# Block attention and a top-1 mixture of experts on one core: where a head pair's two value steps stand in its string of TensorE phases

## The chip, the core and the metric

The kernel runs on one core of a Trainium2 chip. The metric is the device time of one execution in microseconds (us), lower is better. Engines are named as the profile names them: PE is TensorE's matrix multiply and PEld its weight load, DVE is VectorE, ACT is ScalarE, POOL is GpSimd, SP is SyncE, which here only issues transfers. PSUM is the memory that PE writes and that DVE and ACT empty.

## The reference

```
scores = q @ k.T / sqrt(64)                     # 8 batches, 8 heads, 576 positions, depth 64
scores = where(block_i >= block_j, scores, -1e9)       # blocks of 64
attn   = exp(scores - max) / (sum + 1e-9)
x      = (attn @ v), heads side by side          # 4608 tokens x 512
e      = argmax(x @ w_gate);  gate = softmax(x @ w_gate)[e]
eom    = sigmoid(x @ w_output_gate)
out    = gate * eom[e] * (relu(x @ w1[e]) @ w2[e])     # 8 experts, 512 -> 1024 -> 512
```

## The kernel before

The program has two stages. The first, up to about 340 us, is the attention; the second multiplies the sorted tokens by the experts' weights and isn't touched by the change.

The attention goes over 32 head pairs (8 batches, 4 pairs of heads each, `hp` 0 to 3). The work of one pair runs through three turns of the function `attend`: in its first turn the scores and their exponentials, in the next the turning (transposing) of the exponentials, in the third the product with the values. So one call of `attend` works on three pairs at once, and a string of letters sets the order in which PE gets their pieces. PE's order is taken as the code issues it, but for pieces whose buffer the scheduler sees as still taken, behind which it may let the next ones pass. DVE, ACT and POOL get the order that a list scheduler makes of the rest.

- **S** is a step of `softmax`, for the newest pair. Four steps: S1 has query tiles 0 and 1, S2 tile 2, S3 tile 3, S4 the last tile of both heads. Each writes scores into a buffer of the pool `ps_s` (two buffers, each two banks of PSUM; L356 scores, L364 mask, L406 for S4). DVE then takes the maximum (L375), ACT the exponential (L368, for S4 L412). A `ps_s` buffer is free again when its last exponential has been taken, so S1 uses the buffer of the S3 before it, S3 that of S1, S2 that of S4, S4 that of S2.
- **F** is a step of `flip`, for the pair before. F1 to F3 each turn sixteen 64x64 pieces into the pool `ps_f` (one buffer of two banks, L436); ACT and DVE copy one bank each to `pT` (L439). F4 turns two pieces (L460) into a buffer of the pool `ps_t`, which ACT copies (L461).
- **V** is a step of `values`, for the pair before that. V1 multiplies the first two key tiles (L474, eight matmuls that fill one buffer of `ps_t`); V2 the other two, and the last query tile into another buffer of `ps_t` (L474, L487). ACT then copies the one (L481), DVE the other (L491).
- **t** is a tick of `finish_batch`, which normalises a finished batch, writes its rows and routes its tokens (L499 to L689). Its pieces also go through `ps_t`, which has only two buffers, in turn. A batch's ticks spread over four calls, which I name by the `hp` of their newest pair (that of S): in the pair with hp 2 the two parts of the gate's product (L538, copied by ACT at L542), in that with hp 3 rows and logits (L510, L513, L554, L555), in hp 0 three more blocks of rows, in hp 1 the ranks (L638 to L655).
- **.** is the pair's other work: it issues loads, splits of q and k on POOL, and the transposing transfers on SP (L163) which make `qk`, the operand of the scores three pairs on.

Of the kernel before, what the change touches and what calls it, by code (L numbers as in the profile page):

```python
# [26 lines left out]
def block_attention_top1_moe(  # L27
# [12 lines left out]
    B, H, S, D = q.shape  # L40
# [388 lines left out]
    def flip(probs, pT):  # L429

        def group(c0, srcs):
            ps = two_banks()
            for i, src in enumerate(srcs):
                for h in range(2):
                    rows = slice(64 * h, 64 * h + 64)
                    nc.tensor.transpose(ps[:, h, 64 * i:64 * i + 64], src[rows], ident[rows, rows])  # L436
            to = pT.rearrange("p h (s c) -> p h s c", c=P)[:, :, c0:c0 + 10:3]
            one, other = (
                copy(to[:, h], ps[:, h].rearrange("p (s c) -> p s c", c=P))  # L439
                for h, copy in enumerate((nc.scalar.copy, nc.vector.tensor_copy))  # L440
            )
            tc.add_to_no_dep_group(f"turned{one.ins.name}", one.ins)
            tc.declare_no_dep(other.ins, group=f"turned{one.ins.name}", reason="halves in separate banks")

        def keys(pt, j):
            return pt[:, P * j:P * j + P]

        def both(t, n):
            return [keys(probs[t][:, ab], j) for j in range(n) for ab in range(2)]

        pl = probs[LAST]
        group(3, both(3, 4))
        yield
        group(2, both(2, 3) + [keys(pl, 2), keys(pl, 3)])
        yield
        group(1, both(1, 2) + [pl[:, S0:S0 + P], keys(pl, 3), keys(pl, 0), keys(pl, 1)])
        yield
        ps = ps_t.tile([P, 512], F32, name="ps_t")
        for i, src in enumerate(both(0, 1)):
            nc.tensor.transpose(ps[:, P * i:P * i + P], src, ident)  # L460
        nc.scalar.copy(pT[:, :, 0:P].rearrange("p h (a n) -> p a h n", a=2), ps[:, 0:2 * P].rearrange("p (a h n) -> p a h n", a=2, h=2))  # L461
        yield

    def values(hp, pT, vv, vl, xT):

        a0 = 2 * hp
        pa = ps_t.tile([P, 512], F32, name="ps_t")
        for j0, j1 in ((0, 2), (2, LAST)):
            for j in range(j0, j1):
                for ab in range(2):  # L470
                    o = slice(64 * ab, 64 * ab + 64)
                    x = turned_at(j, j)
                    m = LAST - j
                    nc.tensor.matmul(  # L474
                        pa[o, P * j:S0].rearrange("p (t h n) -> p t h n", h=2, n=64), vv[:, j, a0 + ab],
                        pT[:, :, x:x + P * m].rearrange("p h (t n) -> p t h n", n=P)[:, :, :, o],
                        start=(j == 0), stop=(j == LAST - 1),
                    )
            if j0 == 0:
                yield  # L480
        nc.scalar.copy(xT[:, hp, 0:S0], pa)  # L481
        pm = ps_t.tile([P, 512], F32, name="ps_t")
        for j in range(NT):
            for ab in range(2):
                o = slice(64 * ab, 64 * ab + 64)
                x = turned_at(j, LAST)
                nc.tensor.matmul(  # L487
                    pm[o, 0:64], vv[:, j, a0 + ab] if j < LAST else vl[:, a0 + ab], pT[:, ab, x:x + 64],
                    start=(j == 0), stop=(j == LAST),
                )  # L490
        nc.vector.tensor_copy(xT[:, hp, S0:S], pm[:, 0:64])  # L491
        yield
# [584 lines left out]
    def step(g, n=1):  # L1077
        for i in range(n):
            next(g, None)

    def attend(soft, extra=None):

        nxt, flipped, valued = [], iter(()), iter(())
        if flips:
            hp, b, probs, sums, xT, vab = flips.pop()
            pT = sb.tile([P, 2, NPT], F32, name="pT")
            nxt = [(hp, b, pT, vab, sums, xT)]
            flipped = flip(probs, pT)
        if prods:
            hp, b, pT, vab, sums, xT = prods.pop()  # L1090
            valued = values(hp, pT, *vab, xT)
        else:
            hp = None
        def tick():
            for g in list(later):
                if next(g, later) is later:
                    later.remove(g)

        turns = iter(range(4))
        with tc.manual_schedule(engines=ENG):  # L1100
            for x in "S.F.SVFSV.FttSFtt.":
                if x == "S":
                    step(soft)
                elif x == "V":
                    step(valued)
                elif x == "F":
                    step(flipped)
                elif x == "t":
                    tick()
                elif extra is not None:  # L1110
                    extra(next(turns))

        if hp == NP - 1:
            later.append(finish_batch(b, *sums, xT))
        prods.extend(nxt)
# [4 lines left out]
    for p in range(NPR):  # L1120
# [42 lines left out]

        probs = {}
        attend(softmax(p, *sums, probs), others)
        flips.append((hp, b, probs, sums, xT, values_of[b]))
        if p == CP:
# [22 lines left out]
    ps_t.release()  # L1190
    ps_t = ctx.enter_context(tc.tile_pool(name="ps_y", bufs=4, space=PSUM, reuse_waits="tile"))
    attend(iter(()), both_x)
    hp, b, pT, vab, sums, xT = prods.pop()
    ended = values(hp, pT, *vab, xT)
# [126 lines left out]
```

## Time and profile before

| | |
|---|---|
| three runs | 765.82 us in the median (763.86 to 768.5) |
| the profiled execution | 760.66 us, span of its instructions 759.1 us |
| PE busy over the span | 710.0 us, 94% |
| DVE, ACT, POOL busy | 522.8, 489.9, 317.2 us (69%, 65%, 42%) |
| mean granted TensorE clock | 0.994 of full |

Busy time of PE is time in which at least one matmul is in flight. The 1.6 us between the span and the execution's own time lie outside the instructions.

### The profile page before, as it was taken

The page shows a single profiled execution, that of the slowest core. Times are in us where ns is not written, and L with a number is a line of the kernel's source. Part 1 is how long each engine was busy: PE and PEld are TensorE (multiplying, and loading weights), DVE is VectorE, ACT ScalarE, POOL GpSimd, SP SyncE. Part 2 cuts the span into 40 slices and gives each one's busy share as a digit, 9 for nine tenths or more (in the row PEclk, how much of TensorE's full clock was granted, in tenths as well). Part 3 has the DMA queues.
Part 4 walks back from the last instruction along what each step waited for, and adds up shares of the span by engine and source line. Part 5 has one row for each costly group of instructions (what it writes and reads, how often), then busy time and mean ns, then how long its engine had stood idle before and what let it go on. Part 6 is the DMA issues. An engine that isn't in the chain of part 4 may idle for free. (4 is left out here: it accounts for less than half of the span.)

```text
span 759.1 us, 20344 instructions
## 1 busy us (share of the span) xinstructions
PE 710.0 (94%) x7967; PEld 498.6 (66%) x7990; DVE 522.8 (69%) x873; ACT 489.9 (65%) x1081; POOL 317.2 (42%) x377
## 2 busy tenths in 40 slices
PE   6989899999998999988999999999999999999994
PEld 4766576767776676656577666667666666766661
DVE  5866777878786878787849657765576665766630
ACT  4877687878787787854348656656566566566530
POOL 4091669677675783135365224132123232110111
PEclk9999999999999999999999999999999999999998
DMA  6979999998999996369565885947899679623501
GB/s 161 170 142 211 199 223 171 168 195 164 218 163 196 181 160 163 108 220 235 109 146 120 276 263 126 287 128 243 253 315 283 145 225 294 100 37 101 191 30 44
DMA packets 238359, 136.04 MB, mean 179 GB/s; under 512 B 194096, under 2 KB 210544, under 8 KB 238256
## 3 DMA queue, kind: packets, MB, share of 16 engines
q1 hardware_dynamic: 229440, 115.11, 67.2%
q0 software_dynamic: 8272, 19.29, 8.4%
q8 instruction: 65, 1.06, 0.7%
q14 instruction: 38, 0.31, 0.2%
q10 hardware_dynamic: 544, 0.26, 0.1%
HBM read 122.23 MB, written 19.73 MB: 187 GB/s over the span
## 5 line engine op out<-in xcount | busy, mean ns | idle before, releaser
L1035 PEld LDWEIGHTS <-w1b 128*128 128x128 f16 (+1 forms) x2112 | 182.5, 98 | 26.1 <-issue 3.0
L1035 PE MATMUL ps_s<-xt,w1b 128*128 128x256 f16 (+3 forms) x1824 | 182.1, 261 | 0.5 <-DVE w1b L920 0.4
L1062 PE MATMUL ps_t<-w2b,hh 128*128 128x512 bf16 (+1 forms) x585 | 175.9, 379 | 0.0
L920 DVE TENSOR_TENSOR w2b<-w2f,w2b 128x1024 bf16<-128x1024 f32 x76 | 88.0, 1220 | 114.6 <-ACT w2b L918 114.6
L375 DVE TENSOR_REDUCE nmx<-ps_s 128x1 f32<-128x512 f32 (+4 forms) x224 | 130.4, 618 | 17.6 <-PE ps_s L364 14.7
L368 ACT ACTIVATE pt<-ps_s,nmx 128x256 f32<-128x256 f32 (+3 forms) x256 | 131.9, 535 | 8.8 <-DVE nmx L375 8.7
L1066 POOL DMA_INDIRECT out_dram<-ys,ids x38 | 45.4, 1195 | 181.8 <-ACT ys L1065 118.1
L1062 PE MATMUL ps_t<-w2b,hl 128*128 128x512 f16 x304 | 115.2, 379 | 2.1 <-DVE hl L1044 1.0
L1065 ACT ACTIVATE ys<-ps_t,ids 128x512 f32<-128x512 f32 x38 | 26.1, 687 | 135.0 <-PE ps_t L1062 115.5
L1062 PEld LDWEIGHTS <-hh 128*128 128x128 f16 x608 | 59.2, 98 | 66.8
L356 PE MATMUL ps_s<-qk 64*128 64x256 f16 (+1 forms) x1152 | 74.8, 255 | 17.0 <-DMA qk<-sp 11.0
L920 DVE TENSOR_TENSOR w1b<-w1f,w1b 128x1024 bf16<-128x1024 f32 x76 | 88.1, 1218 | 0.0
L439 DVE COPY pT<-ps_f 128x512 f32<-128x512 f32 x93 | 63.9, 688 | 33.5 <-PE ps_f L436 33.5
L474 PE MATMUL ps_t<-pT,vv 128*64 128x256 f32 (+3 forms) x512 | 83.8, 448 | 2.0 <-DVE xn L513 2.0
L918 ACT CAST w1b<-w1f 128x1024 f16<-128x1024 f32 x76 | 74.1, 1045 | 0.5 <-DMA w1f<-in_moe_w_dram 0.5
L887 POOL DMA_INDIRECT xg<-x_d,ids x38 | 53.1, 1397 | 49.8 <-DVE xr L1001 14.9
L918 ACT CAST w2b<-w2f 128x1024 f16<-128x1024 f32 x76 | 73.6, 1042 | 0.0
L356 PEld LDWEIGHTS <-qk 64*128 64x128 f16 x1152 | 50.2, 95 | 29.6 <-DMA qk<-sp 13.6
L439 ACT COPY pT<-ps_f 128x512 f32<-128x512 f32 x93 | 55.5, 596 | 19.3 <-PE ps_f L436 18.6
L436 PEld LDWEIGHTS ps_f<-ident,pt 64*128 64x128 f32 x1116 | 42.7, 139 | 25.0 <-issue 13.1
L436 PE MATMUL ps_f<-ident,pt 64*128 64x64 f32 x1116 | 54.6, 231 | 3.7 <-DVE pT L439 2.3
L689 POOL DMA_INDIRECT tab_d<-idg,sli x40 | 41.0, 1025 | 36.7 <-DVE sli L658 17.3
(213 smaller groups left out, 992.4 us busy)
## 6 DMA issues: line engine op xcount, KB each, us to landing
w1f<-in_moe_w_dram SPq DMA_DIRECT2D x76, 512.0 KB
w2f<-in_moe_w_dram SPq DMA_DIRECT2D x76, 512.0 KB
vv<-in_v_dram SPq DMA_DIRECT2D x64, 128.0 KB
x_d<-xn SPq DMA_DIRECT2D x32, 256.0 KB
natk<-in_k_dram SPq DMA_DIRECT2D x14, 512.0 KB
natq<-in_q_dram SPq DMA_DIRECT2D x28, 256.0 KB
hh<-in_moe_w_dram SPq DMA_DIRECT2D x4, 512.0 KB
hl<-in_moe_w_dram SPq DMA_DIRECT2D x4, 512.0 KB
```

The costliest lines, as they stand in the source:

```text
L356: nc.tensor.matmul(ps[:, ab, c:c + m], qk[rows, cq, P * t:P * t + P], cols(qk[rows, ck], x, kind), start=(i == 0), stop=(i == 2 and c + m ...
L368: last_exp[0] = nc.scalar.activation(probs[t][:, ab], ps[:, ab, c0:c0 + n], AF.Exp, bias=nmx[:, t, ab:ab + 1], accum_out=sums[:, t, 2 * hp ...
L375: last_max[0] = nc.vector.tensor_reduce(o, x, AX.X, ALU.max, negate=True)
L436: nc.tensor.transpose(ps[:, h, 64 * i:64 * i + 64], src[rows], ident[rows, rows])
L439: copy(to[:, h], ps[:, h].rearrange("p (s c) -> p s c", c=P))
L474: nc.tensor.matmul(pa[o, P * j:S0].rearrange("p (t h n) -> p t h n", h=2, n=64), vv[:, j, a0 + ab], pT[:, :, x:x + P * m].rearrange("p h ( ...
L887: nc.gpsimd.indirect_dma_start(out=xg[i % NXG][:, h], out_offset=None, in_=x_d[0:nx, :], in_offset=IOA(ap=ids[i][:, h, 0:1].bitcast(U32), ...
L918: nc.scalar.copy(hi, src)
L920: eng.tensor_tensor(lo, src, hi, ALU.subtract)
L1035: nc.tensor.matmul(ph[:, f4].rearrange("p (h n) -> p h n", n=P), wv[:, cc, f, :], xv[:, cc], start=(k == 0), stop=(k == 3 * KD - 1))
L1062: nc.tensor.matmul(py, hv[:, f, h], wv[:, f, :], start=(k == 0), stop=(k == 3 * KF - 1))
L1066: nc.gpsimd.indirect_dma_start(out=out, out_offset=IOA(ap=ids[i][:, h, 0:1].bitcast(U32), axis=0), in_=ys, in_offset=None, bounds_check=NT ...
```

## The change

The string in `attend` is another. Each step is issued as often as before; the order of S, F and V changes, and with it the four places of the other work.

```diff
-            for x in "S.F.SVFSV.FttSFtt.":
+            for x in "SF.VSF.VSF.ttSFtt.":
```

With their numbers the phases are, before and after:

```
S1 . F1 . S2 V1 F2 S3 V2 . F3 t t S4 F4 t t .
S1 F1 . V1 S2 F2 . V2 S3 F3 . t t S4 F4 t t .
```

On PE, in the middle of a pair, the program before has the end of S2's mask, V1, F2, and the start of S3 (`pt` and `plast` are exponentials, `vv` and `vlast` values):

```order
L364 LDWEIGHTS mrow
L364 MATMUL ps_s<-mneg,mrow 128x2x32
L474 MATMUL ps_t<-pT,vv 64x512 x2
L474 MATMUL ps_t<-pT,vv 64x384 x2
L436 MATMUL ps_f<-ident,pt_3192 128x64 x12
L436 MATMUL ps_f<-ident,plast_115 128x64 x4
L356 LDWEIGHTS qk
L356 MATMUL ps_s<-qk 128x256
```

The changed program has at this place the end of S2's mask, F2, the whole of V2, and the start of S3:

```order
L364 LDWEIGHTS mrow
L364 MATMUL ps_s<-mneg,mrow 128x2x32
L436 MATMUL ps_f<-ident,pt_3193 128x64 x12
L436 MATMUL ps_f<-ident,plast_115 128x64 x4
L474 MATMUL ps_t<-pT,vv 64x256 x2
L474 MATMUL ps_t<-pT,vv 64x128 x2
L487 MATMUL ps_t<-pT,vv 64x64 x8
L487 MATMUL ps_t<-pT,vlast_106 64x64 x2
L356 LDWEIGHTS qk
L356 MATMUL ps_s<-qk 128x256
```

V1 went from behind S2 to ahead of it, V2 from behind S3 to ahead of it; F2 follows S2 at once.

On DVE, in the pair with hp 3, the program before has F2's copy, S3's maxima, V2's copy, F3's copy, two pieces of the tick and S4's maximum:

```order
L439 COPY pT<-ps_f 128x4x128
L375 TENSOR_REDUCE nmx<-ps_s 128x1 x2
L491 COPY xT<-ps_t 128x64
L439 COPY pT<-ps_f 128x4x128
L513 TENSOR_TENSOR xn<-ps_t,rec 64x512
L555 TENSOR_TENSOR lh<-ps_t,rec 128x512
L375 TENSOR_REDUCE nmx<-ps_s 128x1
```

The changed program has there:

```order
L439 COPY pT<-ps_f 128x4x128
L491 COPY xT<-ps_t 128x64
L375 TENSOR_REDUCE nmx<-ps_s 128x1 x2
L439 COPY pT<-ps_f 128x4x128
L513 TENSOR_TENSOR xn<-ps_t,rec 64x512
L555 TENSOR_TENSOR lh<-ps_t,rec 128x512
L375 TENSOR_REDUCE nmx<-ps_s 128x1
```

Only V2's copy moved, ahead of S3's maxima; F3's copy and the tick's pieces still stand behind these maxima.

On DVE in the pair with hp 2 (L683 is a reciprocal that waits for POOL, L502 a small copy of the tick) the piece of the difference is:

```order
+L491 COPY xT<-ps_t 128x64
+L375 TENSOR_REDUCE nmx<-ps_s 128x1 x2
+L439 COPY pT<-ps_f 128x4x128
+L502 COPY sums<-ps_t 64x4
 L683 RECIPROCAL idg<-zs 128x5
-L491 COPY xT<-ps_t 128x64
-L439 COPY pT<-ps_f 128x4x128
-L502 COPY sums<-ps_t 64x4
 L546 RECIPROCAL rec<-rec 128x40
 L375 TENSOR_REDUCE nmx<-ps_s 128x1
```

The reciprocal that waits for POOL stands behind F3's copy and L502 now, and no longer ahead of V2's copy. ACT's order is the same in both programs in the steady pairs, POOL's throughout; on SP one store of rows changes places with one transposing transfer.

## Rows read from the trace of the kernel before

**Rows 1.** Busy us by stretch, one batch: length, engines' busy us, PEclk, DMA share, GB/s.

```profile
165.00:203.00 38.00, 36.97 (x607) 26.91 (x606) 30.82 (x63) 30.78 (x99) 27.21 (x38) 1.00 1.00 188
```

**Rows 2.** The waits of PE, whole span: waiting <- releaser: us in total, times, longest.

```profile
PE ps_s L356 <- DMA qk<-sp: 11.0, 7, 2.6
```

**Rows 3.** Timeline of PE, pair hp 3: start us, us, line, op.

```profile
158.59 0.67 PE L356 MATMUL ps_s<-qk 64*128 64x256 f16 x12
...
159.22 1.72 PE L474 MATMUL ps_t<-pT,vv 128*64 128x512 f32 x8
160.88 0.59 PE L436 MATMUL ps_f<-ident,pt 64*128 64x64 f32 x12
...
161.42 0.82 PE L356 MATMUL ps_s<-qk 64*128 64x256 f16 x12
162.08 0.19 PE L364 MATMUL ps_s<-mneg,mrow 64*128 64x64 bf16 x2
162.20 0.87 PE L474 MATMUL ps_t<-pT,vv 128*64 128x256 f32 x8
...
163.58 0.46 PE L436 MATMUL ps_f<-ident,pt 64*128 64x64 f32 x8
...
164.22 0.62 PE L510 MATMUL ps_t<-ident,xT 128*64 128x128 f32 x4
...
165.12 0.91 PE L406 MATMUL ps_s<-qk 128*128 128x256 f16 x9
165.86 0.41 PE L460 MATMUL ps_t<-ident,pt 128*128 128x128 f32 x2
166.21 0.28 PE L356 MATMUL ps_s<-qk 64*128 64x128 f16 x3
```

**Rows 4.** Timeline of DVE, the same pair.

```profile
162.31 1.29 DVE L375 TENSOR_REDUCE nmx<-ps_s 128x1 f32<-128x512 f32 x2
...
164.33 0.69 DVE L439 COPY pT<-ps_f 128x512 f32<-128x512 f32 x1 [0.41 <-PE ps_f L436]
164.94 0.67 DVE L513 TENSOR_TENSOR xn<-ps_t,rec 64x512 f32<-64x512 f32 x1
```

**Rows 5.** Timeline of PE, pair hp 0: F2 and S3.

```profile
171.20 0.59 PE L436 MATMUL ps_f<-ident,pt 64*128 64x64 f32 x12 [0.48 <-DVE pT L439]
...
172.16 0.83 PE L356 MATMUL ps_s<-qk 64*128 64x256 f16 x12 [0.24 <-ACT pt L368]
```

**Rows 6.** Timeline of PE behind pair hp 1: S1 and S2 of the next.

```profile
185.72 0.34 PE L356 MATMUL ps_s<-qk 64*128 64x128 f16 x6
...
187.25 0.67 PE L356 MATMUL ps_s<-qk 64*128 64x256 f16 x12 [0.28 <-ACT plast L412]
```

**Rows 7.** Timeline of PE, first pair: S3's mask, then the next pair's S1.

```profile
15.10 0.21 PE L364 MATMUL ps_s<-mneg,mrow 64*128 64x64 bf16 x2
...
17.73 0.34 PE L356 MATMUL ps_s<-qk 64*128 64x128 f16 x6 [0.77 <-ACT pt L368]
```

**Rows 8.** Timeline of all engines, pair hp 2: S3, its first exponential, L542, second L538.

```profile
151.95 0.82 PE L356 MATMUL ps_s<-qk 64*128 64x256 f16 x12
...
154.13 0.69 ACT L368 ACTIVATE pt<-ps_s,nmx 128x512 f32<-128x512 f32 x1
...
156.10 0.58 ACT L542 COPY lgT<-ps_t 128x512 f32<-128x512 f32 x1
...
157.06 0.32 PE L538 MATMUL ps_t<-xT,wg_bd 128*32 128x64 f32 x8
```

**Rows 9.** Timeline of PE, three stretches: the longest waits after 110 us.

```profile
116.84 1.07 PE L538 MATMUL ps_t<-xT,wg_bd 128*32 128x512 f32 x8 [1.22 <-DVE xT L491]
...
245.18 0.28 PE L356 MATMUL ps_s<-qk 64*128 64x128 f16 x3 [2.57 <-DMA qk<-sp]
...
265.54 0.34 PE L356 MATMUL ps_s<-qk 64*128 64x128 f16 x6 [0.79 <-DMA qk<-sp]
```

**Rows 10.** Timeline of POOL, pair hp 3: a split that waits for a transfer.

```profile
164.57 0.72 POOL L152 CAST sp<-natq 128x640 f16<-128x640 f32 x1 [3.51 <-DMA qk<-sp]
```

## The prediction

> **What bounds the kernel now.** I read the stretches first: one batch of the attention, four pairs, takes 38.0 us, of which PE is busy 36.97, DVE 30.8 and ACT 30.8 [rows 1]. In the middle of the attention PE is all but full, and what can be won there is about 1 us a batch. Then the waits of PE: the largest is S1 waiting for its `qk`, 11.0 us in seven places [rows 2]. Two of them are the S1 rows at 245.18 and 265.54 us [rows 9]; the other five lie in the first 100 us and take 11.0 - 2.57 - 0.79 = 7.6 us together. There a transfer sets the time, not PE's order. Then the timeline of PE, for the length of each phase as the difference of starts: S2 0.63, V1 1.66, F2 0.54, S3 0.78, V2 1.38, F3 0.64, the tick ahead of S4 0.9, S4 0.74, F4 0.35 [rows 3]. Last DVE and ACT, for how soon a buffer of PSUM is empty again.
>
> The second stage, from about 345 us on, is PE-bound and keeps its order; I carry it over unchanged. So the sum is over the attention alone.
>
> **What the change moves.** No instruction is added or removed, and V1 and V2 still lie between the same two F's. So the distance from F1 to F2 and from F2 to F3, which must cover the copies out of the single `ps_f` buffer, stays as it is. What changes is when S2 and S3 end: S2 by V1's 1.66 us later, S3 by V2's 1.38 us later, while F3, S4, F4 and the ticks stay in place. Behind S3's last matmul there used to be V2; now F3, S4, F4 and the next S1 and F1 follow with nothing between that needs no quick emptying.
>
> *S1 behind S3.* S1 takes S3's buffer. In the first pair no V has begun yet, and the trace shows the new order's spacing: S3's mask ends at 15.10 + 0.21 = 15.31, and S1 starts at 17.73 after a wait for ACT [rows 7]. So about 2.4 us must lie between. In the changed order S3's mask ends 0.85 us after S3 starts and F3 starts at 0.78; F3, S4 and F4 then take 0.64 + 0.74 + 0.35 = 1.73, so PE reaches S1 1.66 us after the mask [rows 3]. A tick between them adds 0.9 in hp 3 and as much or more in hp 0 and hp 2: enough there. In hp 1 the tick is a few small matmuls, and S1 waits. Bounds: 0 (the ranks' matmuls and a faster DVE fill it) to 0.76; I take 0.45, since DVE in the first pair was also busy with other work. Against this S2 has V1 ahead of it now and no longer waits for S4's exponential: the 0.28 of [rows 6] goes. Sum for hp 1: **+0.2**.
>
> The Trainium skill (Perfetto Trace Analysis, "Optimizing Tensor Performance") asks that independent matmul groups go round different PSUM banks, so that ACT or DVE empties one while the next group runs. The changed order still does so: S3 in one `ps_s` buffer, F3 in `ps_f`, S4 in the other `ps_s`, F4 in `ps_t`. By this rule alone every copy stays hidden, none of the waits of this part comes, and the sum is that of the faster rival below. The first pair's row goes round the same way and waits all the same, because the way round is shorter than the emptying; where they differ I go by the row.
>
> *F4 and the ticks behind S3's maxima, hp 3.* DVE's two maxima of S3 take 1.29 us, start 0.04 after the mask, and F3's copy stands behind them. Now that copy starts when F3 ends, 0.75 after F3's start (164.33 against 163.58) [rows 3, 4]. In the changed order it starts at 0.85 + 0.04 + 1.25 = 2.14 after S3's start, that is 1.36 after F3's: 0.6 later. The L513 behind it ends at 164.94 + 0.67 = 165.61 now; with some 0.15 for the signal F4, which needs that buffer of `ps_t`, could start at 165.76 and does at 165.86 [rows 3, 4]. The slack is 0.1, so F4 comes 0.5 late. The scheduler has let one matmul of S1 pass F4, and the two further ticks come behind S1. Bounds 0 and 0.6; I take **+0.4**.
>
> *hp 0.* S3 waits 0.24 for S1's exponentials, and starts 0.96 after F2 where 0.54 is the rule [rows 3, 5]. V2 between them ends this: -0.4. The wait of F2 for its copy (0.48) stays: DVE only swaps S1's maxima with a reduction of the tick, with the same sum ahead of F1's copy. Two blocks of rows then wait as in hp 3, +0.4. Sum: **0**.
>
> *hp 2.* The gate's second L538 needs the buffer that ACT empties at L542. L542 ends at 156.68, L538 starts at 157.06: slack 0.38 [rows 8]. S3's first exponential starts 2.18 after S3 now, behind V2's copy; it can start at 0.85 + 0.65 + 0.1 = 1.6 in the changed order, so with S3 1.38 later ACT's row comes 0.8 later. 0.8 - 0.38 = 0.42, and a little for the signal: **+0.5** (bounds 0, and 1.0 if ACT gains nothing). In the first batch the reciprocal that waits for POOL stood ahead of V2's copy and cost L538 1.22 us [rows 9]; it now stands behind what L538 needs. That place then has only the new wait: **-0.6**.
>
> A steady batch so costs 0.2 + 0.4 + 0 + 0.5 = +1.1 us.
>
> **The sum.** Up to about 100 us the five other waits for `qk`, 1.5 us in the mean, follow each other pair by pair, so what PE loses or gains there is swallowed. From there to the S1 at 245.18: hp 1 of the first batch +0.2, hp 2 -0.6, three batches at 1.1, hp 3 +0.4, together +3.3. That S1 waited 2.57 us for its transfer [rows 9], which I take to come when it came: +0.7 is left. The pairs up to 265.54 add 0.2, and the 0.79 waited there leaves 0.1. Behind it no `qk` is waited for: hp 2 +0.5, hp 3 +0.4, hp 0 nothing (DVE has the ticks' arithmetic there), hp 1 without a tick +0.3, hp 2 +0.5, the last hp 3 +0.4. The last `attend` follows DVE's work, which is the same; there the change puts F3 ahead of a step that waits for a load, -0.1. Total 0.1 + 2.0 = **+2.1 us**, on the profiled 760.66 that is 762.8. The median of the runs shown is 5.2 us above that execution, so I forecast 767.9, 0.3% above 765.82. The measurement can tell about 0.5%, 3.8 us, from no change: the forecast is "same", on the slow side.
>
> **Rivals.**
> - *The new waits are not swallowed, and F3 gets one in each pair (slower).* F2's copy on ACT now stands behind S2's exponentials, which are 1.66 us later. From S2 to F3 there are 0.63 + 0.54 + 1.38 + 0.78 = 3.33 us [rows 3]. The chain for S3's tile is 0.85 to the mask's end, 0.65 for one maximum, two exponentials at 0.68, 0.6 for a copy, some 3.5; S2's tile is a quarter narrower, so about 3.1. The slack is 0.2 in all of some 26 pairs. It decides when a copy or a small piece of a tick pushes ACT 0.2 us back: each further 0.2 costs 5 us. Besides, the transfers may come later too: POOL's splits wait for small results of DVE that now stand behind S4's maximum, up to 3 us later by the same working, against the 3.51 us that POOL waits for a transfer's end anyway [rows 10]; if these don't hide it, the 3.4 us swallowed above come back. For it: both margins are thin. Against it: both are positive in the rows. Time: 767.9 + 3.4 to 5 = 771 to 773.
> - *The gains stay and the late copies are hidden (faster).* hp 0 -0.4, hp 1 -0.28, over five batches, and the 1.22 of [rows 9]: -4.6 us, part of which turns into waits for `qk`. Time about 762. Against it: the slack of 0.1 at F4 and of 0.38 at L538 are far below the 1.38 us by which S3 comes later.
> - *The transfers alone set the pace.* A `qk` arrives 2.57 us late for 245.18; if all S1 from 165 us on are nearly bound by it, neither loss nor gain shows before the last 60 us: +2 or less, within the forecast's range of 765 to 770. The new order of SP is one swap and can't move it much.
>
> **Chances.** The forecast and the transfers' case 0.55 together, the slower rival 0.35, the faster 0.10. Range: from the faster rival's 762 to 774, the slower one's 773 and a little for the part of its waits that I couldn't bound; the likeliest case alone has 764.5 to 770.5. Faster by over 0.5% 0.09, within 0.5% 0.55, slower by over 0.5% 0.36.
>
> **What would show it.** In the profile after: a wait of S1 for ACT behind hp 1 (0.3 to 0.7 us), of F4 or the ticks for DVE in hp 3 and hp 0, of L538 for ACT in hp 2; the waits of rows 5 (S3's), 6 (S2's) and the 1.22 of rows 9 gone; the waits for `qk` at the places of 245 and 265 us smaller by what PE lost before; V's and F's lengths unchanged and the second stage as long as now. The prediction is wrong if F3 waits for ACT in most pairs, if DVE's F3 copy is not later against F3, or if the waits for `qk` move by more than PE's own delay.

## The result, and the profile after

The changed kernel takes 774.44 us in the median of four runs (772.06 to 776.32), the kernel before 765.58 (763.86 to 768.50): the ratio is 1.011 (1.0068 to 1.0152), slower by more than the 0.5% that can be told from no change. The forecast was 767.9, the range 762 to 774. In four more measurements of the same two kernels, in which both ran on the same chip, the ratio is 1.0070 (1.0037 to 1.0103) on a first chip, 1.0043 (1.0010 to 1.0076) and 1.0040 (1.0010 to 1.0070) on a second, and 1.0110 (1.0063 to 1.0156) on a third. What sets the third apart is the main finding below. The ratios leave out slow runs, more than 1.5% over the fastest of the same kernel, so they lie a little off those of the medians, which are of all runs. On which chip the first measurement's runs took place isn't known; three of its four runs of the kernel before were there ahead of the prediction, the fourth, 765.33 us, came with the result.

The profiled execution takes 772.06 us, its span is 770.4. Busy times of the whole span, and the stretch that answers to [rows 1] (length, busy us of PE, PEld, DVE, ACT, POOL, PEclk, DMA share, GB/s):

```profile
PE 718.9 (93%) x7990; PEld 504.8 (66%) x7990; DVE 517.3 (67%) x873; ACT 489.7 (64%) x1081; POOL 321.1 (42%) x377
...
165.00:203.00 38.00, 36.75 (x596) 26.70 (x594) 30.06 (x62) 30.36 (x98) 27.68 (x38) 1.00 1.12 193
```

A batch in the middle looks nearly as before: PE is busy 36.75 of 38 us, where it was 36.97. What the change did there is seen in single waits. The waits of PE over the whole span (compare [rows 2]: us in total, times, longest):

```profile
PE ps_s L356 <- ACT pt L368: 8.1, 10, 2.1
PE ps_s L356 <- DMA qk<-sp: 6.7, 5, 2.0
...
PE ps_s L356 <- issue: 1.9, 5, 0.5
...
PE ps_f L436 <- DVE mx L573: 1.4, 5, 0.3
PE ps_t L538 <- DVE sums L502: 1.2, 1, 1.2
...
PE ps_s L1035 <- issue: 1.0, 3, 0.4
```

The kernel before has, of these:

```profile
PE ps_s L356 <- ACT pt L368: 2.6, 7, 0.8
...
PE ps_s L356 <- issue: 0.2, 1, 0.2
```

S1 and S3 now wait 8.1 us for ACT, not 2.6; less is waited for `qk`; and there are rows that the kernel before hardly has: "issue", where PE stands still and no wait is recorded.

The timeline of PE in the pair with hp 3, from S3 on (before: [rows 3]), then of DVE there (before: [rows 4]):

```profile
164.03 0.83 PE L356 MATMUL ps_s<-qk 64*128 64x256 f16 x12
...
164.72 0.44 PE L436 MATMUL ps_f<-ident,pt 64*128 64x64 f32 x8
...
166.24 0.91 PE L406 MATMUL ps_s<-qk 128*128 128x256 f16 x9
167.15 0.21 PE L356 MATMUL ps_s<-qk 64*128 64x128 f16 x1
167.46 0.44 PE L460 MATMUL ps_t<-ident,pt 128*128 128x128 f32 x2
```

```profile
164.93 1.29 DVE L375 TENSOR_REDUCE nmx<-ps_s 128x1 f32<-128x512 f32 x2 [0.56 <-PE ps_s L364]
166.13 0.68 DVE L439 COPY pT<-ps_f 128x512 f32<-128x512 f32 x1
166.73 0.67 DVE L513 TENSOR_TENSOR xn<-ps_t,rec 64x512 f32<-64x512 f32 x1
```

F3's copy starts 166.13 - 164.72 = 1.41 us after F3, where it was 0.75; F4 starts 1.22 after S4, where it was 0.74, with a matmul of S1 ahead of it. The other places, in PE's timeline: the second L538 in hp 2, F2 in hp 0 (before: [rows 5]), S1 behind hp 1 ([rows 6]):

```profile
119.85 0.32 PE L538 MATMUL ps_t<-xT,wg_bd 128*32 128x64 f32 x8 [0.25 <-ACT lgT L542]
...
172.56 0.34 PE L436 MATMUL ps_f<-ident,pt 64*128 64x64 f32 x4 [0.27 <-DVE mx L573]
...
187.65 0.34 PE L356 MATMUL ps_s<-qk 64*128 64x128 f16 x6 [0.47 <-ACT pt L368]
```

S3's wait of [rows 5], S2's of [rows 6] and the 1.22 of [rows 9] are gone, as foretold. No F3 waits for ACT.

**Where the time went in this execution.** S4 of pair 27 starts 1.0 us later than before (283.63 against 282.62), S4 of pair 31 6.8 us later, the end 11.3 us later. So the loss between these two profiles stands at the end of the attention and behind it. In PE's timeline of pair 29:

```profile
304.45 0.35 PE L487 MATMUL ps_t<-pT,vlast 128*64 128x64 f32 x4 [0.39 <-issue]
305.17 0.41 PE L356 MATMUL ps_s<-qk 64*128 64x256 f16 x4 [0.36 <-issue]
305.92 0.27 PE L356 MATMUL ps_s<-qk 64*128 64x256 f16 x1 [0.34 <-issue]
306.64 0.38 PE L356 MATMUL ps_s<-qk 64*128 64x256 f16 x3 [0.45 <-issue]
307.36 0.27 PE L356 MATMUL ps_s<-qk 64*128 64x256 f16 x1 [0.34 <-issue]
308.06 0.39 PE L356 MATMUL ps_s<-qk 64*128 64x256 f16 x3 [0.43 <-issue]
```

One to four matmuls come every 0.72 us, although nothing is waited for: PE halts. The same is seen at L1035 from 352.2 to 353.6. The granted clock falls behind the halts of pair 29, and again in the hand-over to the experts (windows as above):

```profile
304.00:306.00 2.00, 0.91 (x12) 0.50 (x9) 0.69 (x1) 0.70 (x3) 1.44 (x2) 1.00 0.02 1
306.00:308.00 2.00, 0.83 (x5) 0.13 (x4) 0.00 (x0) 0.00 (x0) 1.95 (x3) 1.00 0.02 1
308.00:310.00 2.00, 1.94 (x26) 1.58 (x27) 1.71 (x4) 1.35 (x4) 0.81 (x1) 0.66 0.00 0
310.00:312.00 2.00, 2.00 (x22) 1.42 (x22) 1.16 (x2) 1.90 (x6) 0.00 (x0) 0.50 0.00 0
...
366.00:368.00 2.00, 0.39 (x5) 0.26 (x3) 2.00 (x4) 0.10 (x1) 1.70 (x2) 0.66 1.04 381
368.00:370.00 2.00, 2.00 (x16) 1.81 (x16) 1.15 (x2) 0.00 (x0) 0.98 (x2) 0.50 1.30 317
370.00:372.00 2.00, 2.00 (x20) 2.00 (x19) 1.77 (x3) 0.00 (x0) 0.00 (x0) 0.50 0.87 117
```

PE had been busy 0.91 and 0.83 us of 2 ahead of the first fall, and 0.39 of 2 ahead of the second. Then it worked at 0.5, which is 1.2 GHz, for 3.4 us from 308.6 on and for 6.8 us from 366.6 on. In the profile of before the clock is full in both places. Is this the change's doing?

### The profile page after: what moved, and what is told of

It is laid out like the page before. It is cut to its first block, busy times and chain, and to the rows that moved or that the text cites. A ratio compares the mean times of both kernels' runs of the same rounds, so it can differ in the third digit from the quotient of the medians.

```text
span 770.4 us, 20390 instructions
## 1 busy us (share of the span) xinstructions
PE 718.9 (93%) x7990; PEld 504.8 (66%) x7990; DVE 517.3 (67%) x873; ACT 489.7 (64%) x1081; POOL 321.1 (42%) x377
## 5 line engine op out<-in xcount | busy, mean ns | idle before, releaser
L1035 PEld LDWEIGHTS <-w1b 128*128 128x128 f16 (+1 forms) x2112 | 184.5, 99 | 27.5 <-issue 4.3
L1035 PE MATMUL ps_s<-xt,w1b 128*128 128x256 f16 (+3 forms) x1824 | 182.1, 261 | 0.3 <-DVE w1b L920 0.2
L1062 PE MATMUL ps_t<-w2b,hh 128*128 128x512 f16 x608 | 180.8, 379 | 0.0
L368 ACT ACTIVATE pt<-ps_s,nmx 128x256 f32<-128x256 f32 (+3 forms) x256 | 132.3, 530 | 43.4 <-DVE nmx L375 41.6
L1062 PE MATMUL ps_t<-w2b,hl 128*128 128x512 f16 x304 | 115.2, 379 | 1.2 <-DVE hl L1044 1.2
L1062 PEld LDWEIGHTS <-hh 128*128 128x128 f16 x608 | 59.2, 98 | 66.8
L356 PE MATMUL ps_s<-qk 64*128 64x256 f16 (+1 forms) x1152 | 78.3, 256 | 18.7 <-ACT pt L368 8.1
L356 PEld LDWEIGHTS <-qk 64*128 64x128 f16 x1152 | 46.7, 95 | 51.3 <-issue 35.6
L887 POOL DMA_INDIRECT xg<-x_d,ids x38 | 56.2, 1480 | 42.9 <-issue 15.0
L439 ACT COPY pT<-ps_f 128x512 f32<-128x512 f32 x93 | 54.4, 585 | 12.9 <-PE ps_f L436 11.3
L689 POOL DMA_INDIRECT tab_d<-idg,sli x40 | 41.0, 1025 | 46.7 <-DVE idg L683 19.7
L1043 ACT ACTIVATE hh<-ps_s 128x1024 f16<-128x1024 f32 (+1 forms) x44 | 39.7, 905 | 27.0 <-PE ps_s L1035 25.0
```

The source lines that it names most:

```text
L356: nc.tensor.matmul(ps[:, ab, c:c + m], qk[rows, cq, P * t:P * t + P], cols(qk[rows, ck], x, kind), start=(i == 0), stop=(i == 2 and c + m ...
L368: last_exp[0] = nc.scalar.activation(probs[t][:, ab], ps[:, ab, c0:c0 + n], AF.Exp, bias=nmx[:, t, ab:ab + 1], accum_out=sums[:, t, 2 * hp ...
L887: nc.gpsimd.indirect_dma_start(out=xg[i % NXG][:, h], out_offset=None, in_=x_d[0:nx, :], in_offset=IOA(ap=ids[i][:, h, 0:1].bitcast(U32), ...
L1035: nc.tensor.matmul(ph[:, f4].rearrange("p (h n) -> p h n", n=P), wv[:, cc, f, :], xv[:, cc], start=(k == 0), stop=(k == 3 * KD - 1))
L1062: nc.tensor.matmul(py, hv[:, f, h], wv[:, f, :], start=(k == 0), stop=(k == 3 * KF - 1))
```

## Experiments

In all that follows a *step* is the time from S4 of one pair to S4 of the next. Theory: the loss is made behind pair 26. Rival: each pair costs. Second rival: halts and late transfers come by chance or with the chip, and the change itself costs 2 to 4 us.

**The changed kernel again**, on the first chip and on the third.

> The changed kernel once more. If what its profile shows behind 300 us belongs to the program (matmuls that come in small groups from 304.4 to 308.1 us with nothing to wait for, and then the clock at 0.5 up to 312; the clock at 0.5 again from 367 to 373), a second profile has both at the same places and the ratio is again 1.007 to 1.015. If they were chance, the profile lacks them and the time is 4 to 8 us lower.

> The changed kernel a third time, on the chip of these runs. If its loss is what the steps between pairs show, +3 to +4 us (1.004 to 1.005); if it is the 8.9 us of the first measurement, 1.010 to 1.013.

On the first it gave 769.16 against 765.00 us, ratio 1.0070, and its profile has no halt in pair 29 and none at L1035. (It has one stall that no other profile shows: S1 of pair 18 waits 1.90 us at 187.9, and the clock is at half for 3.4 us from 188.8 on.) On the third it gave 778.74 against 772.23, ratio 1.0110: of the two cases expected there, the 8.9 us of the first measurement came and not the 3 to 4 us of the steps. On this chip the kernel before is slower too, and the profile has the halts of pair 29 again:

```profile
307.85 0.35 PE L487 MATMUL ps_t<-pT,vlast 128*64 128x64 f32 x4 [0.37 <-issue]
308.56 0.48 PE L356 MATMUL ps_s<-qk 64*128 64x256 f16 x5 [0.36 <-issue]
310.00 0.41 PE L356 MATMUL ps_s<-qk 64*128 64x256 f16 x4 [0.94 <-issue]
```

**The string in one part only.** `p` is the number of the call.

```diff
+            for x in "SF.VSF.VSF.ttSFtt." if p < 26 else "S.F.SVFSV.FttSFtt.":    # steady_only; late_only has >= 26
```

> The new string in the calls of attend for pairs 0 to 25, the old one in the last seven calls. Theory 'the end of the attention': the steady pairs cost some 0.55 us a batch, the wait for qk at pair 24 swallows it, and the loss is made behind it, so the time is that of the kernel before, +0 to +2 us (ratio 1.000 to 1.003). Rival 'every pair costs': +6 to +8 us (1.008 to 1.011).

> The old string for pairs 0 to 25, the new one in the last seven calls. Theory 'the end of the attention': +7 to +10 us (1.009 to 1.013), with the halting matmuls near pair 29 and the two stretches at half clock in the profile. Rival 'every pair costs': +2 us (1.002). If the halting hangs on where POOL's scatters fall against PE and these are moved by what came before, it is missing here and the time is +2 to +5.

Measured 1.0051 (1.0009 to 1.0093) and 1.0025 (0.9993 to 1.0057). The theory that the loss is made behind pair 26 falls: it wanted 1.009 or more of the second, and the halts of pair 29 and L1035 are missing from both profiles. The first lies between its two expectations; which part costs more can't be told from these two intervals.

**Parts of the change.**

```diff
-            for x in "S.F.SVFSV.FttSFtt.":
+            for x in "SF.SVF.SVF.ttSFtt.":    # dots_alone
+            for x in "S.F.VSFSV.FttSFtt.":    # v1_alone
+            for x in "S.F.SVFVS.FttSFtt.":    # v2_alone
```

> The old order of S, F and V with the other work at the new places (behind F1, F2 and F3). Theory: the places of the other work move no PE time, 0 to +1 us (1.000 to 1.002). Rival: the loss comes with the other work (the moved transfers and reciprocals), then +5 us or more.

> Only V1 is moved ahead of S2; V2, S3 and the other work stay where they were before. If the new waits all come from V2's place, as the prediction has it, none of them appears: no wait of S1 for ACT behind hp 1, none of the second L538 in hp 2, and S2's wait for plast behind hp 1 (0.28) is gone; a step from S4 to S4 is that of the kernel before or 0.3 us shorter, the time -1.5 to 0 us (0.998 to 1.000). Rival: it is V1's place (S2 and its exponentials 1.66 us later, ACT late for F2's copy and for S1's buffer): +0.5 us a batch or more stays, +3 us.

> Only V2 is moved ahead of S3 (the places of the other work as before). If the waits come from V2's place: S1 behind hp 1 waits about 0.46 for ACT, the second L538 about 0.25, S2 behind hp 1 still its 0.28 for plast; a steady batch costs 0.65 us of the whole change plus 0.3 of V1's lost gain, about +0.9 us; the time +3 to +6 us (1.004 to 1.008). Rival: the waits need both moves; then a batch costs under 0.3 us and the time is +0 to +2.

The first ran on the first chip, the other two on a fourth. Ratios: the other work alone 1.0017 (0.9985 to 1.0049) and V1 alone 0.9999 (0.9975 to 1.0023), both as expected; V2 alone 1.0099 (1.0070 to 1.0129), above the 1.004 to 1.008 expected, though its interval reaches down to it. The steps of a steady batch are sharp enough to part the terms, since on the first, second and fourth chip they repeat within 0.05 us wherever no transfer is late (the third chip: see below). The table has differences of steps between pairs 11 and 23, where no transfer was late, from those of the profiles with the old order:

| step | what lies in it | predicted | change | V1 alone | V2 alone |
|---|---|---|---|---|---|
| hp 3 to hp 0 | F4 in hp 3, F2 and S3 in hp 0 | 0.0 | -0.15 | 0.00 | -0.16 |
| hp 0 to hp 1 | late rows of hp 0 | +0.4 | +0.40 | 0.00 | +0.41 |
| hp 1 to hp 2 | S1 and S2 behind hp 1 | +0.2 | +0.06 | -0.46 | +0.48 |
| hp 2 to hp 3 | the second L538 | +0.5 | +0.25 | -0.22 | +0.49 |
| sum | a steady batch | +1.1 | **+0.56** | -0.7 | +1.2 |

The two parts add up to the whole change, step by step, within 0.1 us. So the new waits come from V2's place, as predicted, and V1's place gives 0.7 us a batch back. V2 alone has both the new wait of S1 and the old one of S2, and the one of L538; V1 alone has none of the three (PE's timelines of pair 14 in V2 alone):

```profile
150.25 0.34 PE L356 MATMUL ps_s<-qk 64*128 64x128 f16 x6 [0.47 <-ACT pt L368]
151.73 0.67 PE L356 MATMUL ps_s<-qk 64*128 64x256 f16 x12 [0.23 <-ACT plast L412]
160.26 0.32 PE L538 MATMUL ps_t<-xT,wg_bd 128*32 128x64 f32 x8 [0.26 <-ACT lgT L542]
```

V1's gain is more than S2's wait of 0.28. From F1 to S3 of the pair with hp 2 the kernel before takes 190.08 - 186.28 = 3.80 us (pair 18, with that wait), V1 alone 152.43 - 149.10 = 3.33 (pair 14):

```profile
186.28 0.69 PE L436 MATMUL ps_f<-ident,pt 64*128 64x64 f32 x16
...
190.08 0.82 PE L356 MATMUL ps_s<-qk 64*128 64x256 f16 x12
```

```profile
149.10 0.69 PE L436 MATMUL ps_f<-ident,pt 64*128 64x64 f32 x16
...
152.43 0.82 PE L356 MATMUL ps_s<-qk 64*128 64x256 f16 x12
```

The other 0.2 us is closer spacing, which hp 3 shows without any wait: S2 starts 0.72 us after F1 and V1 0.14 after S2's mask in the old order; V1 starts 0.62 after F1 and F2 0.03 after the mask in V1 alone. In the first batch V1 alone loses 1.3 us (steps of 11.07 and 10.12 to pairs 10 and 11, where the old order has 10.77 and 9.16): there L538 waits 1.69 us for V2's copy, as V2 hasn't moved.

The moved other work costs PE 1.8 us in the step to pair 1 and 0.9 in that to pair 2, and the changed kernel loses 4.0 us there (steps of 10.59 and 12.99 us in its first profile, where the old order has 8.88 and 10.70). By S4 of pair 8 nothing of it is left: 96.6 to 97.6 us in the five profiles of the changed kernel, 96.7 to 98.0 in six of the old order.

**Is a loss of PE swallowed by late transfers?**

```diff
-            scores(pX, t, 0)
+            [scores(pX, t, 0) for rep in range(14 if p == 19 and t == 3 else 1)]    # late_pe9; late_pe has 5
```

> The kernel before, with the scores and mask of S3 of pair 19 computed five times over (3.1 us more PE work there, the result the same), to see whether PE's delay is swallowed by the wait for qk at pair 24. The prediction's step (the transfer comes when it came): SP issues the transposing transfers behind 215 us at the times of before, pair 24's S1 starts at the time it had, and the whole time is +0 to +1 us. Rival (the transfers follow PE, since SP's queue holds the stores of rows that wait for the ticks): SP's transfers are 3 us later, S4 of pair 22 to the transfer's start 8 to 9.4 us as in the other profiles, the delay stands behind pair 24, and the time is +3 us (1.004).

> The scores and mask of S3 of pair 19 computed fourteen times over in the kernel before (13 x 0.69 = 9 us more PE work, the result the same). If SP's queue runs at its own pace, S1s behind pair 19 find their qk there, the waits for qk behind it vanish, and the time is +3 to +6 us. If the transfers follow PE's work, +8 to +9 us.

The smaller addition makes the step to pair 19 2.7 us longer (11.90 for 9.16), not 3.1; 1.1 us of it is seen in the time (1.0014, 0.9982 to 1.0046: -1.4 to 3.5 us), which tells neither expectation from the other. Of the 9 us 4.4 are seen (1.0057, 1.0019 to 1.0096: 1.5 to 7.4 us), as expected if the transfers don't follow PE: some of PE's loss is covered. The profile of the larger delay has no wait for `qk` behind pair 9 at all, ahead of pair 19 too, where the delay can't be the reason. Where such waits fall differs from one execution to the next: before_a and before_b, two more profiles of the unchanged kernel on the second chip, have in the stretch from 100 to 300 us (waits of PE; before_a first), where [rows 9] have 2.57 and 0.79:

```profile
PE ps_s L356 <- DMA qk<-sp: 10.8, 6, 2.9
```

```profile
PE ps_s L356 <- DMA qk<-sp: 4.1, 2, 2.9
```

**Without most loads of v.** The products from batch 2 on take the values of batches 0 and 1, and with other tokens sent to other experts the second stage is another and longer; only the attention and the pair's difference are used.

```diff
     def load_v(b):
-
+        if b > 1: values_of[b] = values_of[b - 2]; return
```

> The kernel before without the loads of v from batch 2 on (their products take the values of batches 0 and 1): SP's queue, which has no idle stretch from about 120 to 300 us, has 9 issues a batch fewer. If the late transfers of qk (0 to 3.4 us in one to four places, at other pairs in each profile) come from a full queue, they are gone behind pair 10 and the time falls by 3 to 6 us, to 759 to 762, with a smaller spread. If they come from elsewhere (POOL's splits, the transfers' own length), the waits stay and the time is 763 to 766.

> The changed kernel with the same loads left out, so beside the run above it shows what PE's order costs where no transfer is late. By the steps from S4 to S4 in the profiles (0.6 us a batch from pair 10 on, -1.2 at pair 10, +1.5 in the last pairs) it is +3 us over the run above (1.004). If the change's loss comes by way of the transfers (they come later, or starve PE), it is 0 to +1 us. If the steady waits were as large as predicted (1.1 us a batch and the end), +5.

936.87 and 943.32 us. Behind 100 us neither profile has any wait for `qk`, as expected if they come from a full queue, with 9 issues a batch taken from it; but late_pe9, with all loads, has none either, so two profiles don't prove it. From S4 of pair 10 to that of pair 28 they take 175.1 and 177.3 us, the latter with one stall of 2.0 us in the step to pair 13 (F2 waits 1.47 us for DVE) that no other profile has there. Without the stall 0.2 us are left, where the table's steps give about 2. Three of the four steps differ as in the table (-0.16, +0.40, +0.06), so late transfers are no part of these. The fourth doesn't: few_v_before takes 9.45 to 9.73 us for it and few_v_after 9.42 to 9.43, because in the old order S2 waits 0.3 to 0.6 us for `plast` in hp 2, which among the profiles with all loads only late_pe9 has up to pair 27. Why is open. 2.7 us of difference stand at pair 31, the other 3.9 behind the first L1062, in the second stage, which the runs don't explain. These two and late_pe9 ran on the third chip, and the old order halts there too, in pair 29 of few_v_before and of late_pe9 (first and second fence, PE's timelines):

```profile
302.54 0.34 PE L487 MATMUL ps_t<-pT,vv 128*64 128x64 f32 x4 [1.07 <-issue]
303.97 0.28 PE L487 MATMUL ps_t<-pT,vv 128*64 128x64 f32 x2 [1.08 <-issue]
```

```profile
311.28 0.34 PE L487 MATMUL ps_t<-pT,vv 128*64 128x64 f32 x3 [1.06 <-issue]
```

**Both kernels side by side on the second chip, twice.**

> The kernel before, for a profile of it on the chip of these runs. If a part of the loss belongs to the chip (PE halting near pair 29 and late in the hand-over, as on one chip with both orders), the halts stand at the same place in this profile and in the one of the changed kernel beside it, or in neither.

> The changed kernel on the same chip. By the steps between S4 and S4 it is 2.5 us behind the kernel before from pair 9 to 31; what the whole time shows beyond that must stand ahead of pair 9, in late transfers or halts, or behind pair 31. If late transfers carry it, the sum of the waits for qk behind pair 9 is 2 to 4 us larger than in the kernel before's profile; if the hand-over does, the time from pair 31's S4 to the end is; if neither, the time is +2 to +4 us.

> The kernel before on the same chip: halts where the run above has them, then a time of 770 to 773 us; otherwise 764 to 766.

> The changed kernel on the chip of this pair of runs. If the halts of PE in pair 29 and at L1035 belong to some chips, this profile and the next both have them or both lack them. Where they are missing, the time is +2.5 to +4.5 us over the kernel before, as on the two chips without them; where they are present, both kernels are slower and the difference is 6 to 9 us.

No halt in pair 29 or at L1035 in any of the four profiles. 768.83 against 765.25 us (before_a itself 764.44), and 768.57 against 766.12 (before_b 763.31): the same kernel twice has the ratio 0.9963 both times (0.9931 to 0.9996 and 0.9926 to 1.0001), so a ratio here is good to about 0.4%, and the change's 1.0043 and 1.0040 are no more than that. Against before_a and before_b it is 4.4 and 5.3 us. The waits for `qk` between 100 and 300 us are 5.7 and 6.6 us in the changed kernel and 10.8 and 4.1 in the old: they don't carry the loss of these profiles.

**What is worth keeping.** V1 ahead of S2 in all calls, the whole new string in the call of pair 10 alone, where V2's copy no longer stands behind L683:

```diff
+            for x in "SF.VSF.VSF.ttSFtt." if p == 10 else "S.F.VSFSV.FttSFtt.":
```

> V1 ahead of S2 in every call, V2 ahead of S3 (the whole new string) only in the call for pair 10. By the steps: V1 alone is 0.5 us a batch shorter from pair 10 on (2.4 us), pair 10's step 1.2 us shorter than before; so -3.5 us ahead of the late transfers, -1 to -3.5 us in the time (0.996 to 0.999). If what PE gains only turns into waits for qk, 0 us (0.999 to 1.001).

1.0007 (0.9978 to 1.0035): by S4 of pair 15 its profile is 2.6 us ahead of the kernel before, but then S1 of pair 16 waits 1.77 and that of pair 20 3.04 us for `qk`. That PE's gain turns into such waits is likely, but not shown: its 5.2 us of them between 100 and 300 us lie inside the old order's 3.4 to 10.8. No version beats the kernel before by what can be measured.

## Why the prediction was off

The time was 0.4 us outside the range. With both kernels on one chip the change costs 5.4 us (2.8 to 7.9) on the first, 3.3 (0.8 to 5.8) and 3.1 (0.8 to 5.4) on the second by the ratios, 4.2, 3.6 and 2.5 by the medians; the forecast was +2.1, to 767.9, and the changed kernel's medians there are 769.16, 768.83 and 768.57.

- **The step that failed** is the base on which the sum stands. "The second stage, from about 345 us on, is PE-bound and keeps its order; I carry it over unchanged" and the end of the attention were taken from one execution without halts, and "The median of the runs shown is 5.2 us above that execution, so I forecast 767.9" took the runs of before for the changed kernel's too. Between S4 of pair 27 and that of pair 31 the sum has +1.2, and the first measurement has +5.8; behind S4 of pair 31 it has 0, and there are 4.5. From S4 of pair 27 to that of pair 31 the profiles take (us):

| | old order | new order |
|---|---|---|
| first and second chip | 40.4 (before_a), 40.4 (before_b) | 41.6 (after_again), 41.6 (after_a), 41.6 (after_b) |
| third chip | 44.4 (late_pe9), 44.4 (few_v_before) | 46.2 (after_third), 46.2 (few_v_after) |
| first measurement | 40.4 | 46.2 |

  The execution recorded for the changed kernel looks like the third chip, that of the kernel before like the others. The halts cost 4.0 us there in the old order and 4.6 in the new, so the order is not their cause and adds 0.6. From S4 of pair 31 to the end the first measurement has 440.6 us against 436.1; on the third chip late_pe9 has 440.2 and after_third 441.1; the profiles from elsewhere have 435.3 to 438.0 with the old order and 436.0 to 439.1 with the new. So some 7 to 9 of the 11.3 us between the two spans, 4.6 in the attention and 2 to 5 behind it, go by these profiles with the chip and not with the change. The part behind it lies in the hand-over: the first L1062 comes 46.6 us behind S4 of pair 31 where it was 41.7 (46.0 in late_pe9, 47.1 in after_third, 41.1 to 44.7 elsewhere, 44.8 and 44.6 in the pair without loads of v), and from there to the first L1062 of the last tile both profiles take 367.9 us. The second stage proper was carried over rightly. The half clock of the hand-over isn't the change's doing: before_a has it for 3.4 us from 365.3 on and late_pe9 for 6.8 us, before_b and after_again not at all.

  That the profile of before in the first measurement came from another chip than that of the changed kernel is likely. It has no halts, and its page lists 7967 matmuls, as do all five of the second chip, where that of the changed kernel lists 7990, as do all seven from other chips with the same matmuls; the two programs have the same number of them. It was not shown, and two numbers stand against the chip as the whole cause. The run of before that came with the result, 765.33 us, lies below all 13 on the third chip (765.57 at the lowest). And with both kernels on the third chip the change costs 8.5 us by the ratio (4.9 to 12.0), 6.5 by the medians, though the halts there cost both orders nearly the same. Why it costs more there than on the first and second chip stays open.
- **A steady batch** costs 0.56 us and not 1.1. V2's terms were sized well: without the 0.28 for V1 the prediction's four terms are 0, 0.4, 0.45 and 0.5, and V2 alone has -0.16, 0.41, 0.48 and 0.49. The term that was mis-sized is V1's gain, set at the 0.28 of S2's wait: V1 alone gives 0.7, of which 0.22 lie in the step from hp 2 to hp 3, where nothing was set. In hp 0 F2's wait, which I had let stand, shrank from 0.48 to 0.27; it is 0.37 in V1 alone and 0.40 in V2 alone, so both moves have a part in it. F4 came 0.48 late, where 0.5 was worked out.
- **The first batch's gain** was larger: the two steps to pairs 10 and 11 are 1.24 shorter and 0.26 longer, together -0.98, forecast +0.2 - 0.6 = -0.4.
- **The end**: from pair 27 to 31 +1.2 us, and predicted was 0.4 in hp 3, 0 in hp 0, 0.3 behind hp 1 and 0.5 in hp 2, also 1.2. But the places are others, and that the sums agree is luck: S1 behind hp 0 waits for ACT, L538 waits 1.20 for DVE where the kernel before waits 0.53, and of the waits of hp 0 there (F2 0.45, S3 0.25, L510 0.80) F2's 0.28 is left and F3 has a new one for DVE, 0.49:

```profile
296.96 0.21 PE L356 MATMUL ps_s<-qk 64*128 64x128 f16 x1 [1.02 <-ACT pt L368]
...
319.85 0.64 PE L538 MATMUL ps_t<-xT,wg_bd 128*32 128x512 f32 x4 [1.20 <-DVE sums L502]
```

- **What is swallowed.** Up to 100 us this held to the letter (4 us lost, none left). Behind it, "that S1 waited 2.57 us for its transfer, which I take to come when it came" took one execution's chance for a fixed time: there are such waits of 0 to 3.4 us at other pairs in each profile. That the waits for `qk` move by more than PE's own delay was one of the signs of being wrong, and it came. It mattered little, since by pair 23 only -0.98 + 3 x 0.56 = +0.7 us was there to be swallowed and not 3.3. Two errors of opposite sign nearly cancel: the steps sum to 0.7 + 0.6 (pairs 24 to 27, -0.15 + 0.40 + 0.06 + 0.25) + 1.2 = +2.5 us. That the +2.1 lies so near to this is luck. On the second chip the steps' 2.5 lies inside both intervals, on the first just below (2.8 to 7.9); what stands above 2.5 on these two the runs can't tell from chance.
- **The rivals.** The slower one's thin margin at F3 (0.2 us) held: behind the first pairs no F3 waits for ACT in the profiles of the changed kernel. That the first measurement, 774.44, lies near its 771 to 773 is no sign for it. The faster one is half true for V1 (-0.7 a batch) and for pair 10, but V2's waits outweigh it. The Trainium skill (Perfetto Trace Analysis, "Optimizing Tensor Performance") asks that independent matmul groups rotate through different PSUM banks, so that the emptying of one overlaps the next group's matmuls. The changed order does so, and S1's 0.47, L538's 0.25 and F4's 0.48 are there all the same: the way round was too short here.

## What to carry to other kernels

A step that is moved ahead of another one helps if the later one was waiting (V1, 0.7 us a batch) and costs if what follows has only just enough time behind it (V2, 1.2 us): price the two moves apart. A wait for a transfer in one profile is not a reserve that a delay can be charged against; look for it in a second profile first. And where a difference of 1% counts, run both kernels on the same chip: here the kernel before took 7 us more on the third chip (772.23 against 765.0 to 766.1), more than the change cost on the first and second.

## What was not expected of the hardware

On the third chip, in all four of its profiles, PE halts at the same two places of the program, in pair 29 and at L1035, with either order: one to five matmuls come every 0.7 us or at twice that distance, and no wait is recorded; in pair 29 the clock is at half for 3.4 us behind it. None of the thirteen profiles known to be from elsewhere, or taken of the kernel before, has them there. In pair 29 POOL is issuing its indirect transfers of L689 meanwhile, as it does on the chips without halts. Whether PE's instructions come late was not tested; the trace shows one transfer of the queue of kind "instruction" just ahead of the halts (at 303.2 us in the first profile of the changed kernel, 8.2 behind S4 of pair 28, 0.97 us long), and after_a, which doesn't halt, has one of the same length at the same place (309.6 us, 8.1 behind it, 0.96). The cause stays open.
